# Loads of 48 rows for each head, gaps zeroed once, and another order of the work list

## The chip, the cores and the metric

The kernel runs on one core of a Trainium2 chip. Its engines work side by side, each through its own queue in order: TensorE (PE in the profile; its weight loads are PEld), VectorE (DVE), ScalarE (ACT), GpSimd (POOL) and SyncE (SP), which here issues most transfers. The metric is the device time of one execution in microseconds (us); the median of several runs counts.

## The reference

Two blocks follow each other. The first is a gated linear recurrence over 768 tokens, for 4 batches of 8 heads of 48 channels:

```python
f = 1.0 / (1.0 + np.exp(-f_logit))
for t in range(S):
    state = f[:, :, t, :, None] * state + np.einsum('bhd,bhe->bhde', k[:, :, t], v[:, :, t])
    y[:, :, t] = np.einsum('bhd,bhde->bhe', q[:, :, t], state)
```

The second takes y as x of shape (4, 768, 384), adds the real part of a Fourier transform over tokens and channels, and a two-layer perceptron on normalized rows:

```python
mixed = np.real(np.fft.fft(np.fft.fft(x, axis=1), axis=2))
u = x + mixed
un = (u - mean(u)) / np.sqrt(var(u) + 1e-06)      # over the channels
return u + np.maximum(un @ w_ch1, 0.0) @ w_ch2     # 384 -> 1536 -> 384
```

## The kernel before

Two heads of one batch make a unit u; there are 16 units, four to a batch. A unit's logits, keys and queries each lie in a buffer of 112 used partitions by 768 tokens (f32): 48 channels of head 0, a gap, and 48 channels of head 1 from partition 64. The buffers are four for logits (`g_t`), three for keys (`k_t`), four for queries (`q_t`), shared in turn by the units; some are parts of one tile called `wide`. Rows 48 to 63 belong to no head, but elementwise work and transposes run over all 112 rows, so something finite must lie there.

`attention` is a generator with 19 to 24 steps for a unit. For units 0 to 3: exponential of the logits on ScalarE (line 411); transposes on TensorE and logarithms on ScalarE (423, 425); running sums as a product with a triangle (433); the exponentials of the sums, g and W (439, 440), the decays te (458); query product (462) and key product (464) on VectorE; scores (472) and their masked copy (476); outputs within a block (631, 648, 652); state increments ds (673); the state scan stt on VectorE (681); its product with the queries (690); the way back to token rows (700 to 717), and the folding of tokens for the transform (739 to 767). Units 4 to 15 make the running sums with a scan on VectorE (449) instead. `keys_turned` (K, line 610) transposes the key products.

The weights arrive as 64-bit numbers in 24 blocks of 128 x 384 (128 x 768 words of four bytes). `fetch` (r, line 348) loads one into one of three buffers called `raw`; `weights` (C) makes single precision of it with one ScalarE, two VectorE and one GpSimd instruction (319, 321, 322, 323). `fnet` (F) is the transform of one batch, H the normalization and transposes, P the two layers of the perceptron: lines 927, 959, 968 and 982 are its products. V and c read weights a second time to look at their sizes, M judges whether the computation must be repeated in a safer form; for these inputs it is not.

The order of everything is written out by hand in `ORDER`, 970 words. Each word emits one step of one generator, or a load: `L1f` loads the logits of unit 1, `L4qv` queries and values of unit 4, a number n is the next step of unit n. As each engine runs its instructions in the order in which they were emitted, the list fixes every engine's queue, SP's included: a load that must wait for its buffer holds back all loads behind it.

How a load is made depends on the unit. For units 0 to 3, logits and queries come as 96 rows in one transfer (head 0, then head 1 from partition 48 on) and 16 more rows in a second one, which put the first 16 channels of head 1 on partitions 96 to 111; head 1 is thus turned by 16 rows, and the rows from 48 to 63 hold a copy. Keys of units 0 to 3 must be turned in the same way and take three transfers of 48, 32 and 16 rows. All loads of the units from 4 on are two transfers of 48 rows. VectorE zeroes rows 32 to 63 of the three key buffers ahead of the first load. The part of the file for the repeated computation (`few[0]` false) has loads of its own that stay.

Of the kernel before, what the change touches and what calls it, by code (L numbers as in the profile page):

```python
# [12 lines left out]
C = 128  # L13
# [11 lines left out]


ORDER = (
# [27 lines left out]
)  # L55


# [33 lines left out]
def kernel(  # L91
# [13 lines left out]
    nc = tc.nc  # L105
    B, HP, _, D, _, S = qkf.shape
# [8 lines left out]
    R = 64 + D  # L115
    ROWS = [slice(64 * r, 64 * r + D) for r in range(2)]
# [23 lines left out]
    few = [True]  # L140
# [7 lines left out]
    g_t = [fixed([128, S + 1], f"g{i}") for i in range(2)] + [wide_t[:, i * (S + 1):(i + 1) * (S + 1)] for i in range(2)]  # L148
    k_t = [fixed([128, S], f"k{i}") for i in range(2)] + [wide_t[:, 2 * S + 2:3 * S + 2]]
    q_t = [fixed([128, S], f"q{i}") for i in range(2)] + [wide_t[:, i * S + 2:(i + 1) * S + 2] for i in range(3, 5)]  # L150
# [72 lines left out]
    v_of, nulled = {}, []  # L223

    def load(u, *names):
# [3 lines left out]
        for name in names:  # L229
# [7 lines left out]
            rows = qkf.rearrange("b h r d i s -> (b h r d) i s")  # L237
            first = 2 * D * u
            if not nulled:
                nulled.extend(k_t)  # L240
                for a in k_t:
                    nc.vector.memset(a[32:64, :S], 0.0)
            if few[0] and (name == "k" or u >= HP):
                nc.sync.dma_start(out=t[:D, :S], in_=rows[first:first + D, i])
                first, turned = first + D, 16 if u < HP else 0
                nc.sync.dma_start(out=t[64:R - turned, :S], in_=rows[first + turned:first + D, i])
                if turned:
                    nc.sync.dma_start(out=t[R - turned:R, :S], in_=rows[first:first + turned, i])
                continue
            nc.sync.dma_start(out=t[:2 * D, :S], in_=rows[first:first + 2 * D, i])  # L250
            nc.sync.dma_start(out=t[2 * D:R, :S], in_=rows[first + D:first + 64, i])
# [968 lines left out]
```

## Time and profile before

| | us |
|---|---|
| median of 3 runs | 510.63 (510.14 to 513.66) |
| profiled execution | 512.57 |
| its span, first to last instruction | 510.8 |
| TensorE busy in the span | 485.5 |
| VectorE busy | 363.8 |
| ScalarE busy | 233.1 |
| GpSimd busy | 89.5 |
| mean granted TensorE clock | 0.993 |

The profiled execution's own time is 1.8 us above its span, and 1.94 us above the median of the runs. Busy times are sums over the whole span; engines overlap, and the share of an engine says nothing about one stage.

### The profile page before, as it was taken

Reading aid. Unit: us, or ns where it says so; the run is one execution under the profiler, and the core shown is the slowest. Engines: PE = TensorE matmul, PEld = TensorE weight load, DVE = VectorE, ACT = ScalarE, POOL = GpSimd, SP = SyncE. Lnnn points to the kernel's source line nnn. Section 1 sums busy time; section 2 is a strip of 40 time slices with the busy share of each in tenths; the row PEclk is TensorE's granted clock in tenths of the full one; section 3 lists DMA queues with packets and bytes.
Section 4 is the critical chain, followed back from the end, with each engine's and each line's share of the span. In section 5 each row is a group of like instructions: output and inputs, shape, how many; then the busy total and the mean of one; then the engine's idle time right before and its main releaser. Section 6 shows DMA issues by size and latency. Waiting matters only on the chain.

```text
span 510.8 us, 13829 instructions
## 1 busy us (share of the span) xinstructions
PE 485.5 (95%) x5806; PEld 450.2 (88%) x5806; DVE 363.8 (71%) x711; ACT 233.1 (46%) x552; POOL 89.5 (18%) x136
## 2 busy tenths in 40 slices
PE   4878889999999999999999999999999999999997
PEld 4766677886798999998998989999999999999997
DVE  2489988999959684585777886777486666558653
ACT  4688678866230541446463554452431413232130
POOL 2126632644222100000031000111000000010100
PEclk9799999999999999999999999999999999999999
DMA  8877946555201101113011112121200331134001
GB/s 225 236 210 192 248 144 206 170 174 155 83 1 47 38 3 37 43 54 103 30 48 37 49 43 59 58 57 41 98 1 15 110 124 63 62 138 143 31 3 38
DMA packets 20075, 46.20 MB, mean 90 GB/s; under 512 B 3489, under 2 KB 6242, under 8 KB 20002
## 3 DMA queue, kind: packets, MB, share of 16 engines
q1 hardware_dynamic: 18898, 41.66, 28.0%
q0 software_dynamic: 1104, 3.54, 1.9%
q8 instruction: 48, 0.79, 0.7%
q14 instruction: 25, 0.20, 0.1%
HBM read 40.47 MB, written 4.72 MB: 88 GB/s over the span
## 4 chain that ended last, share of the span: by engine, by line
PE 87%; DVE 4%; DMA 3%; ACT 2%; issue 2%; POOL 1%; SPq 0%; POOLq 0%; DVEq 0%; ACTq 0%
PE ub L927 26%; PE fx L982 17%; PE fz L982 12%; PE up L959 6%; PE y L631 3%; PE z L804 3%; PE po L968 3%; PE mix L824 2%; PE y L690 2%; PE ds L673 2%; PE sc L472 2%; PE pt L865 2%; DMA raw<-in_w_ch_dram 2%; PE yt L711 1%; PE run L433 1%
## 5 line engine op out<-in xcount | busy, mean ns | idle before, releaser
L936 DVE TENSOR_TENSOR h<-h,ub 128x512 f32<-128x512 f32 x90 | 61.0, 686 | 32.4 <-PE ub L927 24.7
L934 ACT ACTIVATE h<-ub 128x512 f32<-128x512 f32 x60 | 35.6, 593 | 51.9 <-PE ub L927 50.6
L772 POOL DMA_INDIRECT out_dram<-x,place x16 | 21.3, 1332 | 179.8 <-DVE x L1040 124.3
L927 PE MATMUL ub<-wide,w 128*128 128x128 f32 x400 | 49.8, 276 | 1.7 <-DVE wide L899 1.7
L927 PEld LDWEIGHTS ub<-wide,w 128*128 128x128 f32 x400 | 47.3, 192 | 2.4 <-DVE wide L899 1.6
L939 ACT ACTIVATE h<-h 128x512 f32<-128x512 f32 x50 | 31.1, 632 | 35.2 <-DVE h L936 35.2
L982 PE MATMUL fx<-block,h 128*128 128x192 f32 x264 | 46.7, 327 | 0.0
L982 PE MATMUL fx<-w,h 128*128 128x192 f32 x264 | 45.6, 328 | 0.0
L982 PEld LDWEIGHTS fx<-block,h 128*128 128x128 f32 x264 | 43.4, 190 | 0.2
L982 PEld LDWEIGHTS fx<-w,h 128*128 128x128 f32 x264 | 42.6, 190 | 0.2
L927 PE MATMUL ub<-unT,w 128*128 128x128 f32 x320 | 41.0, 275 | 0.0
L927 PEld LDWEIGHTS ub<-unT,w 128*128 128x128 f32 x320 | 38.4, 192 | 0.0
L323 POOL TENSOR_TENSOR w<-w,raw 128x384 uint32<-128x384 uint32 x24 | 27.7, 1161 | 56.7 <-ACT raw L319 18.7
L959 PE MATMUL up<-unT,w 128*128 128x256 f32 x144 | 33.2, 384 | 0.1
L927 PE MATMUL ub<-wide 128*128 128x128 f32 x240 | 31.9, 276 | 0.9 <-DVE wide L899 0.9
L927 PE MATMUL ub<-unT,wide 128*128 128x128 f32 x240 | 32.2, 277 | 0.0
L866 ACT COPY unT<-pt 128x384 f32<-128x384 f32 x24 | 11.4, 476 | 42.2 <-PE pt L865 42.0
L959 PEld LDWEIGHTS up<-unT,w 128*128 128x128 f32 x144 | 26.7, 190 | 4.3 <-DVE x L887 0.4
L927 PEld LDWEIGHTS ub<-wide 128*128 128x128 f32 x240 | 29.4, 192 | 1.2 <-PE ub L927 1.1
L927 PEld LDWEIGHTS ub<-unT,wide 128*128 128x128 f32 x240 | 29.2, 192 | 0.4
L982 PE MATMUL fz<-block,h 128*128 128x192 f32 x132 | 23.5, 328 | 0.0
L476 DVE COPY_PREDICATED at<-causal,sc 128x768 f32<-128x768 uint32 x16 | 16.6, 1040 | 9.3 <-PE sc L472 8.0
(216 smaller groups left out, 1011.4 us busy)
## 6 DMA issues: line engine op xcount, KB each, us to landing
raw<-in_w_ch_dram SPq DMA_DIRECT2D x24, 384.0 KB, 5.1
v<-in_v_dram SPq DMA_DIRECT2D x16, 288.0 KB, 3.8
k<-in_w_ch_dram SPq DMA_DIRECT2D x12, 384.0 KB, 3.6
g<-in_w_ch_dram SPq DMA_DIRECT2D x12, 384.0 KB, 4.1
k<-in_qkf_dram SPq DMA_DIRECT2D x25, 144.0 KB, 3.4
g<-in_qkf_dram SPq DMA_DIRECT2D x20, 144.0 KB, 4.6
q<-in_qkf_dram SPq DMA_DIRECT2D x20, 144.0 KB
wide<-in_qkf_dram SPq DMA_DIRECT2D x11, 144.0 KB, 4.3
```

The costliest lines, as they stand in the source:

```text
L323: nc.gpsimd.tensor_tensor(bits, bits, lo, ALU.add)
L476: nc.vector.copy_predicated(AT, causal[:, :64].bitcast(U32).unsqueeze(1).unsqueeze(1).to_broadcast([128, 2, NCH, 64]), own[:, :, :NCH * 64 ...
L631: nc.tensor.matmul(y[FILL[g], c // 3, c % 3 * C + t.start:c % 3 * C + t.stop], lhsT=vals[rows, o:o + (64 if g == 0 else D)], rhs=weights, ...
L772: nc.gpsimd.indirect_dma_start(out=out.rearrange("b s d -> (b s) d"), out_offset=bass.IndirectOffsetOnAxis(ap=place[:, b, i:i + 1], axis=0 ...
L804: nc.tensor.matmul(z[:, cols], lhsT=src[:, j, lo:hi], rhs=tab[:, t, T % 2, cols], start=(i == 0), stop=(i == len(parts) - 1), skip_group_c ...
L927: nc.tensor.matmul(chains[chain][:, m * 128:(m + 1) * 128], lhsT=block(w)[:, m * 128:(m + 1) * 128], rhs=tokens(a), start=(new and m == 0) ...
L934: nc.scalar.activation(out, got, kind, scale=1.0 if how == "=+" else -1.0)
L936: nc.vector.tensor_tensor(out, out, got, ALU.add if how == "+" else ALU.subtract)
L939: nc.scalar.activation(out, out, AF.Relu)
L959: nc.tensor.matmul(pp[:, :256], lhsT=w1[:, kt, m * 128:(m + 1) * 128], rhs=unT[:, kt], start=(kt == 0), stop=(kt == 2))
L968: nc.tensor.matmul(po[:, :DM], lhsT=h[:, m, t], rhs=w2[:, m], start=(m == 0), stop=(m == NF - 1))
L982: nc.tensor.matmul(out, lhsT=h[:, m], rhs=blocks[i][:, m], start=(start and m == 0), stop=(m == H - 1), skip_group_check=True)
```

## The change

All loads of units (in the normal computation) become two transfers of 48 rows, one for each head, on partitions 0 to 47 and 64 to 111. Head 1 is no longer turned. Rows 32 to 63 of all eleven buffers are zeroed by VectorE, in an order of their own, ahead of the first load.

```diff
             if not nulled:
-                nulled.extend(k_t)
-                for a in k_t:
+                nulled.extend((g_t[0], g_t[1], q_t[0], g_t[2], k_t[1], k_t[0], q_t[1], g_t[3], q_t[2], k_t[2], q_t[3]))
+                for a in nulled:
                     nc.vector.memset(a[32:64, :S], 0.0)
-            if few[0] and (name == "k" or u >= HP):
-                nc.sync.dma_start(out=t[:D, :S], in_=rows[first:first + D, i])
-                first, turned = first + D, 16 if u < HP else 0
-                nc.sync.dma_start(out=t[64:R - turned, :S], in_=rows[first + turned:first + D, i])
-                if turned:
-                    nc.sync.dma_start(out=t[R - turned:R, :S], in_=rows[first:first + turned, i])
+            if few[0]:
+                for r in range(2):
+                    nc.sync.dma_start(out=t[ROWS[r], :S], in_=rows[first + r * D:first + (r + 1) * D, i])
                 continue
```

The list `ORDER` holds the same 970 words, each as often as before, in another sequence throughout. Its beginning, which the prediction speaks of:

```diff
-    "I L1f L0f i L0v E 1 0 0 1 0 0 L0k r C 0 1 1 0 L0q 0 0 1 L2f 2 L1q 0 Z 0 K0 0 0 r 2 2 r 1 L1k 1 L3fk "
-    "L2q 0 0 2 1 0 0 1 3 1 L2k C C 2 L1v 0 3 3 K1 L4fk 0 1 0 2 L3q 3 1 1 1 2 2 4 1 0 1 3 3 3 L3v 1 2 3 2 "
+    "E r i L1f L0f 0 r 1 r L2f 0 1 0 I L0q 2 0 0 1 L0v Z 2 C 0 L0k 0 1 1 L1v L1q 0 L3fk 1 L1k 0 0 K0 C "
+    "L2q C 0 3 2 2 1 0 1 r L2k L3q L4fk 0 2 0 0 K1 3 3 0 1 2 2 3 1 0 1 C 1 3 1 1 2 2 4 1 1 2 3 3 0 1 4 3 "
```

I sets constants on GpSimd, E the triangle, i loads the 128 x 128 identity, Z zeroes the score buffers. In the old list the first P0 is word 220, behind ten C and 146 steps of units; in the new one it is word 214, behind nine C and 144 steps.

## Rows read from the trace of the kernel before

**Rows 1.** The page: busy time of each engine, and the chain by engine.
```profile
PE 485.5 (95%) x5806; PEld 450.2 (88%) x5806; DVE 363.8 (71%) x711; ACT 233.1 (46%) x552; POOL 89.5 (18%) x136
...
PE 87%; DVE 4%; DMA 3%; ACT 2%; issue 2%; POOL 1%; SPq 0%; POOLq 0%; DVEq 0%; ACTq 0%
```
**Rows 2.** Busy time by stretch: start, end, length, engines, clock, transfer share, GB/s.
```profile
0.00:7.18 7.18, 0.00 (x0) 0.00 (x0) 2.09 (x3) 3.15 (x5) 2.96 (x21) 1.00 0.70 193
7.18:28.00 20.82, 18.84 (x297) 16.67 (x297) 7.51 (x10) 14.06 (x32) 3.29 (x12) 0.84 0.92 243
28.00:57.00 29.00, 23.36 (x777) 20.18 (x777) 27.60 (x43) 22.84 (x56) 16.16 (x27) 1.00 0.74 205
57.00:85.00 28.00, 23.57 (x473) 18.97 (x473) 24.70 (x47) 21.38 (x62) 9.88 (x10) 1.00 0.66 187
85.00:507.30 422.30, 419.74 (x4260) 394.37 (x4260) 301.54 (x610) 171.63 (x402) 57.22 (x66) 1.00 0.22 67
507.30:511.00 3.70, 0.03 (x1) 0.00 (x0) 0.36 (x1) 0.00 (x0) 0.00 (x0) 1.00 0.29 86
```
**Rows 3.** The same view in stretches of 2 us around the slow clock.
```profile
14.00:16.00 2.00, 1.43 (x52) 1.26 (x52) 0.97 (x2) 1.61 (x4) 1.22 (x10) 1.00 1.05 323
16.00:18.00 2.00, 1.29 (x20) 0.90 (x9) 1.68 (x2) 1.67 (x4) 0.00 (x0) 0.70 1.03 243
18.00:20.00 2.00, 2.00 (x52) 1.86 (x52) 1.15 (x2) 0.94 (x2) 0.00 (x0) 0.50 1.03 233
20.00:22.00 2.00, 2.00 (x49) 1.72 (x51) 0.00 (x0) 1.62 (x5) 0.00 (x0) 0.50 0.75 194
22.00:24.00 2.00, 2.00 (x39) 1.66 (x32) 0.22 (x1) 1.60 (x4) 0.00 (x0) 0.59 0.84 233
```
**Rows 4.** TensorE's largest wait (28 to 90 us), and P0's first products in the timeline.
```profile
PE y L690 <- DVE stt L681: 4.7, 6, 1.3
...
84.97 1.56 PE L959 MATMUL up<-unT,w 128*128 128x256 f32 x6
```
**Rows 5.** Timeline of VectorE: start, length, line, operation, idle before and releaser.
```profile
1.03 1.50 DVE L242 MEMSET k<- 32x768 f32 x2 [1.03 <-PEq L1206]
...
10.83 0.36 DVE L321 TENSOR_SCALAR w<-raw 128x384 uint32<-128x384 uint32 x1 [7.49 <-DMA raw<-in_w_ch_dram]
...
14.20 0.96 DVE L464 TENSOR_TENSOR g<-W,k 112x768 f32<-112x768 f32 x1 [0.19 <-DVE q L462]
...
23.78 0.76 DVE L681 TENSOR_TENSOR_SCAN stt<-ds,te 112x288 f32<-112x288 f32 x1 [4.18 <-PE ds L673]
26.91 1.04 DVE L476 COPY_PREDICATED at<-causal,sc 128x768 f32<-128x768 uint32 x1 [2.37 <-PE sc L472]
27.84 0.35 DVE L321 TENSOR_SCALAR w<-raw 128x384 uint32<-128x384 uint32 x1
...
30.38 0.95 DVE L462 TENSOR_TENSOR wide<-wide 112x768 f32<-112x768 f32 x1
```
**Rows 6.** Timeline of the first 13 us: SP, ScalarE and TensorE.
```profile
1.26 0.42 SPq L251 DMA_DIRECT2D g<-in_qkf_dram  x1
...
4.25 0.84 ACT L411 ACTIVATE g<-g 112x768 f32<-112x768 f32 x1 [2.15 <-DMA g<-in_qkf_dram]
...
6.20 0.84 ACT L411 ACTIVATE g<-g 112x768 f32<-112x768 f32 x1 [1.01 <-DMA g<-in_qkf_dram]
...
7.18 2.28 PE L423 MATMUL pg<-ident,g 112*128 112x112 f32 x10 [7.18 <-ACT g L411]
...
12.12 0.90 ACT L439 ACTIVATE g<-run,rise 112x768 f32<-112x768 f32 x1 [0.57 <-PE run L433]
```
**Rows 7.** Transfer queues over the whole span: transfers, MB, share.
```profile
q1 hardware_dynamic: 18898, 41.66, 28.0%
```
**Rows 8.** Busy time by stretch while loads of 48 + 48 rows land.
```profile
121.00:122.00 1.00, 1.00 (x20) 0.88 (x16) 1.00 (x3) 0.00 (x0) 0.57 (x1) 1.00 1.03 271
122.00:123.00 1.00, 1.00 (x4) 0.60 (x4) 0.96 (x2) 0.48 (x1) 0.54 (x1) 1.00 1.01 264
```

50 rows, old and new, of the table ORDER are left out of this document.

## The prediction

> **What bounds the kernel now.** I read the page's busy times and its chain first [rows 1]. TensorE is busy 485.5 us of a span of 510.8 us, and 87% of the chain that ended last lies on it. So the time is TensorE's work plus its idle time, and the diff leaves the count and shapes of its matmuls alone: only the 25.3 us of idle time, and the clock at which the work runs, can move. The busy times by stretch [rows 2] say where the 25.3 us lie: 7.18 us before its first instruction; 20.82 - 18.84 = 1.98 us up to 28 us; 29.00 - 23.36 = 5.64 us from 28 to 57 us; 28.00 - 23.57 = 4.43 us from 57 to 85 us; 422.30 - 419.74 = 2.56 us from 85 us to the last product; and some 3.5 us of stores behind it. Nearly all that can be won or lost lies ahead of 85 us, where the first projection (P0) begins, at 84.97 us [rows 4].
>
> Within that, from 28 to 57 us VectorE is busy 27.60 of 29.00 us, and TensorE's largest wait is for VectorE's state scan (stt, line 681), 4.7 us in six places from 28 to 90 us [rows 4]. Between 10 and 28 us VectorE is anything but full (7.51 of 20.82 us): it sits 4.18 us before its first state scan and 2.37 us before the copy at 26.91 us, then runs the vector halves of the second and third weight conversion (C) from 27.84 to 30.38 us, already in its full stretch [rows 5]. The very start waits for loads: ScalarE's first exponential begins at 4.25 us, the second at 6.20 us, and TensorE behind it at 7.18 us [rows 6]. The transfers are nearly saturated there (share 0.92 at 243 GB/s, [rows 2]).
>
> **The change, part by part.** *Bytes and transfers.* Eight loads (logits and queries of the first four units) were 96 + 16 rows and become 48 + 48. Each row is 768 x 4 = 3072 bytes, so 8 x 16 rows = 393 KB go. Four key loads go from three transfers to two at equal bytes. At 243 GB/s the bytes are 1.6 us of a stream that after 28 us no waiting TensorE instruction names; I count them only at the start (below) and otherwise at 0, with -1.6 as the other end. The four transfers saved are four issues of about 0.42 us on SP [rows 6]; nobody was seen waiting for SP's issue itself, so 0.
>
> *Zeroing.* Three fills of 32 x 768 become eleven. Two took 1.50 us [rows 5], so eight more are 6.0 us, from 1.03 us to about 9.3 us. VectorE's next work was at 10.83 us, when a weight block landed, so the cover is idle time and the cost 0; without that cover it would be up to 6 us. The new wait is SP's: a load must wait for its buffer's fill. The first load (logits of unit 1, second in the list of fills) may be issued at 1.03 + 1.50 = 2.53 us instead of 0.81 us, and all that SP holds is queued behind it. But a weight block (128 x 768 words, 393 KB) and the identity (128 x 128 words, 66 KB) are now queued ahead of it, and 459 KB keep the transfer engines past 2.53 us, so this costs nothing on top of the next item (bare, it would be +1.7 us).
>
> *The first loads behind a weight block.* Before, the second logits load (344 KB) landed about 1.95 us after the first (ScalarE starts at 4.25 and 6.20 us, [rows 6]), that is 176 KB per us. 459 KB ahead, less 2 x 49 KB no longer loaded, is 361 KB, or 2.0 us at that rate and 1.5 us at 243. Unit 0's exponential comes first in the new list, but its logits are the second to land, so TensorE starts at about 7.18 + 2.0 = 9.2 us, and the exponentials of the running sums, at 12.12 us before [rows 6], come at about 14. I take **+2.0** (ends +1.5 and +2.5; the nearest row is that of the same two loads).
>
> *Two more blocks before the third logits.* Two further weight blocks are now fetched before unit 2's logits, whose exponential stands ahead of unit 0's second set on ScalarE. By that point 2.13 MB are asked for; at 243 GB/s from about 2.2 us they are there at 11.0 us, while unit 0's logarithms end near 12. Cost 0; the other end is +1.
>
> *Keys of unit 1.* They are now queued on SP behind keys of unit 3, which wait until VectorE has used unit 0's keys (its product, 14.20 us before, ends near 17.2). Two loads of 295 KB then take 2.4 us plus about 2 us to land, so they are there at 21.8 us. In the new list VectorE first does the copy of unit 0, two weight conversions and unit 1's query product, and gets there at about 22. Cost 0, the other end +1.
>
> *What fills VectorE's gap.* In the new list the second and third conversion stand before unit 1's products, that is, in the idle stretch up to 27 us, where 4.18 + 2.37 = 6.55 us were idle. They need only blocks that were fetched at the very start. They took 30.38 - 27.84 = 2.54 us of the full stretch, which then begins earlier: **-2.5** (bounds 0, if the lag eats the gap, and -2.5). Unit 2's query product, 0.95 us at 30.38 us, also moves ahead of unit 1's copy, into the wait for the scores: **-0.95** (bounds 0 and -0.95). What is late next is the state scan of unit 0, whose product on TensorE carries the lag of 2.0 us.
>
> *The rest of the list.* P0 first stands at word 214 instead of 220 of 970, with nine conversions before it instead of ten and 144 attention steps instead of 146. So the stage that keeps TensorE full starts with slightly less done; the work is only deferred. After 85 us the idle time before the tail is 2.56 us [rows 2]; another sequence may lose it or double it: 0, with ends -2.6 and +2.6.
>
> *Sum.* +2.0 - 2.5 - 0.95 = -1.45 us. The profiled execution was 512.57 us with a span of 510.8, so 1.8 us lie around the span: 509.35 of span, 511.1 profiled. The median of the runs shown, 510.63, is 1.94 us below the profiled one, which gives **509.2 us**.
>
> *A rule that speaks against the loads.* In rows, the 96 + 16 loads ran at 243 and 233 GB/s between 16 and 20 us with the transfer engines full [rows 3]. From 121 to 123 us, when 48 + 48 loads of units 8 to 11 are what is left in flight, the rate is 271 and 264 GB/s at full share [rows 8]. So 48-row pieces are not slower. The Trainium skill, page SBUF — State Buffer, section "Door 1: The DMA port swizzle", says that a transfer reaching only partitions 0 to 63 (or only 64 to 127) reaches half of the 16 ports and so half the bandwidth; by it each new piece would go at half rate where a 96-row piece spanned both halves. The trace does not bear that out at these rates.
>
> **The rivals.** *The clock (slower).* The granted clock was 0.70, 0.50, 0.50 and 0.59 in the four stretches from 16 to 24 us: the lower of the two levels, 1.2 GHz, after TensorE had been busy only 1.43 and 1.29 of 2 us; it rose again after it had been busy throughout from 18 us [rows 3]. That is 8 x (1 - 0.57) = 3.4 us of work lost. If the later and sparser start (waits for logits, for the third exponential) gives a second such stretch, or one twice as long, and the lag is not repaid, the time is 510.6 + 2.0 + 3.4 = 516.0. It decides if TensorE is not continuously busy by about 24 us. Against it: the three units in flight then give it as much work as before.
>
> *The lag stays.* Scores, sums and scans of unit 0 all come 2 us later and VectorE's gap only moves: 510.6 + 2.0 = 512.6, up to 514.6 if the keys of unit 1 and the third logits cost 1 us each. For it: VectorE has a single order, and what stands before a late scan cannot pass it.
>
> *The lead grows (faster).* VectorE's full stretch sets TensorE's 5.64 + 4.43 = 10.07 us of idle time from 28 to 85 us. If the new order halves it, on top of the sum's -1.45, the time is 510.6 - 1.45 - 5.0 = 504.2. For it: the largest wait there is for VectorE's scan. Against it: VectorE's work ahead of P0 stays the same but for a conversion, and 27.60 of 29.00 us leave it little to compress.
>
> *Half-rate pieces.* If the 48-row pieces ran at half of 243 GB/s, eight loads of 295 KB would take 19.4 us instead of 8 x 344 KB in 11.3 us: +8 us, in a stretch whose transfers are saturated, so about 518.7 at worst. This is the page's rule put as a mechanism of this kernel; rows 8 speak against it.
>
> *The loads change nothing.* If the old filler rows cost nothing and the zeros hide fully, only the list remains, and that is inside the forecast.
>
> **How the numbers follow.** Forecast (lag repaid, 506 to 512): 0.48. Lag stays (512 to 515): 0.17. Clock: 0.13. Half-rate pieces: 0.02. Lead grows: 0.20. The predicted time is that of the first, 509.2 us. The range leaves out about a tenth on either side, half of the clock case with the half-rate case and half of the faster case: 504.2 to 515.5. A measurement of this kernel tells about 1% (505.5 to 515.7) from no change. Faster by more than that: 0.20, all from the growing lead. Slower: 0.15, the clock and the half-rate pieces. Same: 0.65.
>
> **What would show it.** In the changed profile: eleven fills on VectorE to about 9 us; the first logits exponential near 8 us and TensorE's first instruction near 9.2 us; two conversions on VectorE before its first state scan; VectorE's sum from 28 to 57 us still above 27 us; P0's first matmul (line 959) within 2 us of 84.97 us [rows 4]; queue 1 moving 41.66 - 0.39 = 41.27 MB [rows 7]; 1.2 GHz for no more than about 8 us. The prediction is wrong if P0 begins more than 4 us away from there, or if TensorE's idle time after 85 us moves by more than 3 us: then the sequence, which I could only bound, outweighs the start that I worked out.

## The result, and the profile after

| | before | after |
|---|---|---|
| median, us | 510.87 (508.96 to 515.67, 22 runs) | 513.72 (511.12 to 518.17, 22 runs) |
| ratio, after to before | | 1.005 [1.0028, 1.0072] |
| profiled execution, us | 512.57 | 513.28 |
| its span, us | 510.8 | 511.6 |
| its mean granted clock | 0.993 | 0.989 |

The changed kernel is slower by 0.5%, some 2.6 us (1.4 to 3.7 by the interval). The forecast was 509.2 us, 0.3% faster. The time lies in the range that was given, and within the 1% that was called "same", but on the other side of no change than the sum of -1.45 us. Ratios and means of runs here and below leave out every run more than 1.5% above the fastest of its kernel, among them three that stand far off, at 630.31 us (conversions_back), 712.81 us (before_held) and 2777.74 us (before).

The two profiled executions show only 0.7 of these 2.6 us, since that of before was 1.7 us above its median and that of after 0.4 below. So the traces show what happened in each stretch, and the repeated runs what it cost. Line numbers after are three lower than before (L439 is now L436, L690 is L687, L959 is L956).

The page after, as in [rows 1] and [rows 7]: busy times, the granted clock in 40 slices of 12.8 us, queue 1, and the chain by engine.

```profile
PE 486.4 (95%) x5806; PEld 449.9 (88%) x5806; DVE 366.0 (72%) x719; ACT 233.3 (46%) x552; POOL 87.5 (17%) x136
...
PEclk9799899999999999999999999999999999999999
...
q1 hardware_dynamic: 18706, 41.27, 28.4%
...
PE 84%; ACT 4%; DMA 4%; DVE 4%; issue 2%; SPq 2%; POOL 0%; ACTq 0%; DVEq 0%; POOLq 0%
```

The clock is below full in the second slice and again in the fifth, from 51 to 64 us. Queue 1 moves the 41.27 MB that were forecast; the bytes that went bought nothing that can be seen. The busy times by stretch, in the stretches of [rows 2]:

```profile
7.18:28.00 20.82, 16.04 (x228) 14.12 (x229) 10.69 (x16) 14.62 (x30) 4.06 (x3) 0.84 0.90 233
28.00:57.00 29.00, 25.13 (x830) 21.48 (x829) 25.00 (x41) 23.33 (x60) 13.86 (x17) 1.00 0.74 197
57.00:85.00 28.00, 24.94 (x490) 19.62 (x485) 24.38 (x46) 22.76 (x62) 12.50 (x18) 0.94 0.63 178
85.00:507.30 422.30, 419.50 (x4267) 394.19 (x4266) 300.16 (x613) 171.35 (x402) 51.78 (x67) 1.00 0.23 68
507.30:512.00 4.70, 0.76 (x5) 0.46 (x3) 0.36 (x1) 0.00 (x0) 0.00 (x0) 0.89 0.23 68
```

Read them against [rows 2]. Up to 28 us TensorE does 16.04 us instead of 18.84. From 28 to 57 us VectorE falls from 27.60 to 25.00 us of 29.00, where above 27 was forecast: it is no longer full, it waits. From 57 to 85 us the clock is 0.94, where it was 1.00. TensorE's idle time up to 507.3 us is 7.18 + 4.78 + 3.87 + 3.06 + 2.80 = 21.7 us against 21.8 before, so in this pair idle time was only moved, and the difference is 0.84 us more of busy time, with a mean clock of 0.989 against 0.993. Idle time after 85 us moved by 0.24 us.

The start after, ScalarE's and TensorE's timeline, against [rows 6]: first logits, first transposes, logits of unit 2, exponential of unit 0's sums.

```profile
7.56 0.84 ACT L408 ACTIVATE g<-g 112x768 f32<-112x768 f32 x1 [5.47 <-DMA g<-in_qkf_dram]
...
8.55 2.28 PE L420 MATMUL pg<-ident,g 112*128 112x112 f32 x10 [8.55 <-ACT g L408]
...
13.74 0.84 ACT L408 ACTIVATE wide<-wide 112x768 f32<-112x768 f32 x1 [2.51 <-DMA wide<-in_qkf_dram]
14.58 0.88 ACT L436 ACTIVATE g<-run,rise 112x768 f32<-112x768 f32 x1
```

The exponential of unit 0's sums starts at 14.58 us, 2.46 us later than at 12.12. ScalarE stood 2.51 us for the logits of unit 2, which land at about 13.7 us and not at 11.0. Up to there the transfers ran at 248 GB/s at a share of 0.92, as fast as before (0.92 and 243 GB/s in [rows 2]):

```profile
2.20:13.70 11.50, 4.73 (x24) 4.20 (x24) 7.54 (x12) 3.12 (x7) 3.73 (x22) 1.00 0.92 248
```

VectorE's timeline, against [rows 5]:

```profile
6.68 3.12 DVE L242 MEMSET wide<- 32x768 f32 x4
9.84 0.36 DVE L318 TENSOR_SCALAR w<-raw 128x384 uint32<-128x384 uint32 x1
...
17.35 0.96 DVE L461 TENSOR_TENSOR g<-W,k 112x768 f32<-112x768 f32 x1 [0.90 <-DMA k<-in_qkf_dram]
...
20.40 0.35 DVE L318 TENSOR_SCALAR w<-raw 128x384 uint32<-128x384 uint32 x1
...
21.65 0.56 DVE L319 SCALAR_TENSOR_TENSOR w<-raw,w 128x384 uint32<-128x384 uint32 x1
22.12 0.95 DVE L459 TENSOR_TENSOR q<-q,g 112x768 f32<-112x768 f32 x1
24.10 1.63 DVE L461 TENSOR_TENSOR g<-W,k 112x768 f32<-112x768 f32 x1 [1.03 <-DMA k<-in_qkf_dram]
27.60 0.76 DVE L678 TENSOR_TENSOR_SCAN stt<-ds,te 112x288 f32<-112x288 f32 x1 [1.88 <-PE ds L670]
28.28 0.93 DVE L459 TENSOR_TENSOR wide<-wide 112x768 f32<-112x768 f32 x1
30.50 1.05 DVE L473 COPY_PREDICATED at<-causal,sc 128x768 f32<-128x768 uint32 x1 [1.29 <-PE sc L469]
...
35.20 0.76 DVE L678 TENSOR_TENSOR_SCAN stt<-ds,te 112x288 f32<-112x288 f32 x1 [1.95 <-PE ds L670]
```

The fills end at 9.8 us. The second and third conversion run from 20.40 to 22.2 us, ahead of the first state scan, as forecast. But the first scan comes at 27.60 us instead of 23.78, and with the copy that ends at 30.50 + 1.05 = 31.55 us VectorE has done the same work that it had done at 30.38 + 0.95 = 31.33 us before. What was moved forward has just paid for the lag. Then it stands 1.95 us for unit 1's scan, at 35.20 us: the conversions that filled this place before are used up. The same scan in the kernel before came 1.88 us earlier and hardly waited:

```profile
33.32 0.76 DVE L681 TENSOR_TENSOR_SCAN stt<-ds,te 112x288 f32<-112x288 f32 x1 [0.30 <-PE ds L673]
```

The lag also grows on its way: 1.37 us at the first transposes, 2.46 us at the exponential of the sums, 3.15 us at unit 0's key product (17.35 against 14.20 us) and 3.82 us at the first scan. At the key product VectorE waits 0.90 us for unit 0's keys themselves, for which SP issues the load at 10.49 us, where it was issued at 4.20 us before. In every profile TensorE's first scores start 0.10 us behind this product.

The clock, in stretches of 2 us (columns as in [rows 3]):

```profile
16.00:18.00 2.00, 0.90 (x6) 0.49 (x5) 1.10 (x2) 2.00 (x7) 0.24 (x1) 1.00 0.97 253
18.00:20.00 2.00, 1.14 (x49) 1.03 (x50) 0.84 (x2) 1.91 (x4) 1.18 (x1) 0.87 0.57 161
20.00:22.00 2.00, 2.00 (x45) 1.72 (x48) 1.93 (x5) 1.31 (x3) 0.00 (x0) 0.50 0.98 239
22.00:24.00 2.00, 2.00 (x27) 1.88 (x21) 1.07 (x2) 2.00 (x6) 1.72 (x2) 0.50 0.74 152
24.00:26.00 2.00, 2.00 (x26) 1.75 (x28) 1.63 (x1) 0.55 (x2) 0.91 (x1) 0.50 0.89 300
...
58.00:60.00 2.00, 0.24 (x8) 0.24 (x12) 1.97 (x4) 1.46 (x3) 1.99 (x7) 1.00 0.99 227
60.00:62.00 2.00, 2.00 (x22) 1.12 (x19) 2.00 (x2) 1.05 (x5) 1.77 (x4) 0.61 1.03 235
```

TensorE, busy 0.90 and 1.14 of 2 us, falls to the lower level (1.2 GHz) at about 19.5 us and stays there until about 26.3 us. A second such stretch, new against before, follows a pause at 58 to 60 us, in which it works 0.24 us and waits 1.92 us for a state scan:

```profile
59.76 1.01 PE L687 MATMUL y<-q,stt 48*48 48x128 f32 x20 [1.92 <-DVE stt L678]
```

### The profile page after: what moved, and what is told of

It reads as the page before. It is cut to its first block, busy times and chain, and to the rows that moved or that the text cites. A ratio compares the mean times of both kernels' runs of the same rounds, so it can differ in the third digit from the quotient of the medians.

```text
span 511.6 us, 13832 instructions
## 1 busy us (share of the span) xinstructions
PE 486.4 (95%) x5806; PEld 449.9 (88%) x5806; DVE 366.0 (72%) x719; ACT 233.3 (46%) x552; POOL 87.5 (17%) x136
## 3 DMA queue, kind: packets, MB, share of 16 engines
q1 hardware_dynamic: 18706, 41.27, 28.4%
## 4 chain that ended last, share of the span: by engine, by line
PE 84%; ACT 4%; DMA 4%; DVE 4%; issue 2%; SPq 2%; POOL 0%; ACTq 0%; DVEq 0%; POOLq 0%
PE ub L924 27%; PE fx L979 17%; PE fz L979 12%; PE z L801 4%; PE up L956 4%; PE po L965 3%; PE y L628 3%; PE mix L821 3%; PE y L687 2%; DMA wide<-in_qkf_dram 2%; PE ds L670 2%; PE yt L708 1%; PE sc L469 1%; PE pt L862 1%; PE st L607 1%
## 5 line engine op out<-in xcount | busy, mean ns | idle before, releaser
L769 POOL DMA_INDIRECT out_dram<-x,place x16 | 16.5, 1029 | 210.5 <-DVE x L1037 88.4
L956 PE MATMUL up<-unT,w 128*128 128x256 f32 x144 | 32.7, 383 | 0.6 <-DVE x L884 0.6
L956 PEld LDWEIGHTS up<-unT,w 128*128 128x128 f32 x144 | 26.9, 190 | 4.9 <-PE yt L708 0.8
L863 ACT COPY unT<-pt 128x384 f32<-128x384 f32 x24 | 11.5, 478 | 42.9 <-PE pt L862 42.9
L979 PE MATMUL fz<-w,s 128*128 128x192 f32 x132 | 23.4, 327 | 0.0
```

Source lines behind the costliest of these rows:

```text
L769: nc.gpsimd.indirect_dma_start(out=out.rearrange("b s d -> (b s) d"), out_offset=bass.IndirectOffsetOnAxis(ap=place[:, b, i:i + 1], axis=0 ...
L956: nc.tensor.matmul(pp[:, :256], lhsT=w1[:, kt, m * 128:(m + 1) * 128], rhs=unT[:, kt], start=(kt == 0), stop=(kt == 2))
L979: nc.tensor.matmul(out, lhsT=h[:, m], rhs=blocks[i][:, m], start=(start and m == 0), stop=(m == H - 1), skip_group_check=True)
```

## The experiments

Each ratio is to runs of the kernel before on the same chip, where its medians were 510.39 to 511.13 us in the groups of runs below; the ratio on record isn't the quotient of the medians, and the two differ by up to 0.4%. The theories under test: **A**, the start, the weight blocks ahead of the first and third logits and the lag behind them; **E**, VectorE's gap only moved, so that the moved conversions are worth nothing; **F**, the clock, 1.2 GHz more often because TensorE works more sparsely; **H**, the wait of the first loads for the fills; **I**, the loss lies in the first part of the new list. Where an expectation uses other letters, they stand for rivals that it describes itself.

**The two halves of the change.** loads_alone has the loads and fills of after with the list of before, list_alone the reverse.

```diff
 # loads_alone: lines 237 to 247 of after, ORDER of before
 # list_alone: ORDER of after, load() of before
```

> The new loads and the eleven fills under the old list. Theory A (the cost comes from the new list: two weight blocks ahead of unit 2's logits, and TensorE's pause at 58 us): the loads cost only what the first fill holds back, 1.7 us less 98 KB saved, about +1 us at the start, most of it taken up later: 510.5 to 512 us, ratio below 1.003. Theory B (the loads themselves cost, by a lower rate of 48-row pieces or by the fills): 512.5 us or more, ratio 1.004 or more, with loads of one unit seen to take longer than 344 KB did before.

> The new list with the old loads (96 + 16 rows, three fills). Theory A: slower than before by 2 to 4 us, ratio 1.004 to 1.008, as 393 KB more are moved under the same order; ScalarE waits for unit 2's logits 2.5 us or more at about 11 us. Theory B: no different from before, ratio 0.998 to 1.002.

Measured: 512.78 us, 1.0056 [1.0031, 1.0081], and 515.27 us, 1.0089 [1.0057, 1.0121]. Each half costs, and they don't add up: under the new list, the new loads go with a lower time, 513.7 against 515.27 us. In loads_alone A, by which the loads cost next to nothing, was to give a ratio below 1.003, and failed. Without a weight block ahead of it, the first load's wait for the fills lies open; ScalarE of loads_alone, as in [rows 6]:

```profile
5.95 0.84 ACT L408 ACTIVATE g<-g 112x768 f32<-112x768 f32 x1 [3.85 <-DMA g<-in_qkf_dram]
```

5.95 against 4.25 us is the 1.7 us that the prediction gave as the bare cost of the fills. In list_alone the first exponential starts at 7.50 us, as late as after, so the late start as such belongs to the list. But the logits of unit 2 start ScalarE at 12.43 us after a wait of 1.26 us, where 2.5 us or more were expected, and the exponential of unit 0's sums comes at 13.27 us, later by 1.15 us and not by 2.46.

**Single places of the new list.** logits_first asks for unit 2's logits ahead of the two weight blocks. state_first moves unit 4's steps ahead of unit 3's before word S, so that the scan that TensorE waited for at 59.76 us comes earlier. conversions_back returns the second and third conversion behind unit 1's masked copy.

```diff
 logits_first
-E r i L1f L0f 0 r 1 r L2f 0 1 0 I
+E r i L1f L0f L2f 0 r 1 r 0 1 0 I
 state_first
-K4 7 5 3 3 S 4 4 4 4 6 5 4 F0
+K4 7 4 4 5 4 3 3 S 4 6 5 4 F0
 conversions_back
-K0 C L2q C 0 3 2 2 ... 3 3 0 1 2 2 3 1 0 1 C
+K0 L2q 0 3 2 2 ... 3 3 0 1 2 2 3 1 C C 0 1 C
```

> The changed kernel with unit 2's logits asked for ahead of the two further weight blocks, all else as it is. Theory A: ScalarE's third exponential no longer waits until 13.74 us but starts near 11, unit 0's exponentials of the sums come 1.5 to 2.5 us earlier (14.58 us in the changed kernel), and the time falls by 1 to 2 us, to a ratio of 1.001 to 1.003. Rival C (what is lost at the start is taken up by 57 us anyway, since VectorE then sets the pace): the wait goes and the time stays at 1.005.

> The changed kernel with unit 4's state scan moved ahead of unit 3's folding on VectorE (and its state increments ahead of unit 5's scores on TensorE). Theory A: TensorE's pause from 57.8 to 59.8 us goes or shrinks below 0.5 us, the clock of 0.61 and 0.54 from 60 to 64 us with it, and the time falls by 1 to 2 us, to a ratio of 1.001 to 1.003. Rival D (the pause only moves: what the folding delays is late instead): the time stays at 1.005 and the slow clock turns up elsewhere ahead of 85 us.

> The changed kernel with the second and third weight conversion moved from VectorE's first gap to behind unit 1's masked copy, near where the old list has them. The forecast's step (they cost nothing in the first gap and 2.5 us later): 2 to 2.5 us slower than the changed kernel, ratio 1.009 to 1.010. Theory E (the gap only moved: VectorE idles from 33.2 to 35.2 us in the changed kernel because the work that used to fill it is gone): no slower, ratio 1.003 to 1.007, and VectorE's idle time from 28 to 57 us falls by 1.5 us or more.

Measured: 1.0056 [1.0029, 1.0082], 1.0074 [1.0049, 1.01] and 1.0037 [1.0006, 1.0068]. None is told apart from the changed kernel's 1.005. In logits_first ScalarE did not wait for unit 2's logits (first row), but the exponential of unit 0's sums came at 13.87 us, only 0.71 us earlier where 1.5 to 2.5 were expected. The first scan came at 25.04 us without idle time, 2.6 us earlier; this lead isn't the logits' alone, as the granted clock of this profile is 1.00 up to 28 us, against 0.84 in the profile after. The second scan came where it was, after 4.20 us of idle time:

```profile
11.48 0.84 ACT L408 ACTIVATE wide<-wide 112x768 f32<-112x768 f32 x1
...
25.04 0.76 DVE L678 TENSOR_TENSOR_SCAN stt<-ds,te 112x288 f32<-112x288 f32 x1
...
35.20 0.76 DVE L678 TENSOR_TENSOR_SCAN stt<-ds,te 112x288 f32<-112x288 f32 x1 [4.20 <-PE ds L670]
```

What is won at the first scan is stood off at the next. The trace shows on what: ahead of the second scan TensorE stops for 1.88 us inside a group of scores, and no engine and no transfer of data is named as what released it.

```profile
29.90 0.32 PE L645 MATMUL sc<-q,g 48*64 48x64 f32 x7
32.10 0.47 PE L645 MATMUL sc<-q,g 48*64 48x64 f32 x17 [1.88 <-issue]
```

Such pauses inside a group stand ahead of 60 us in 12 of the 16 profiles, 22 in all, of 0.17 to 2.94 us. In TensorE's stream, products and weight loads counted together, they lie at six positions, 450, 705, 961, 1217, 1473 and 2241 (or the one behind), which are 256 or a multiple of it apart, give or take one. Each ends 1.27 to 1.63 us after a packet of the instruction queue has landed (q8 on the page: 48 packets, 0.79 MB, so 16 KB each). So TensorE most likely stands here for its own program code; that is read from the traces, and no run tests it. The pause above is at position 705. Its packet lands at 30.67 us here and at 31.00 us after, where TensorE gets to that place at 32.36 us and no pause shows. As long as this packet comes when it does, an earlier first scan can't bring the second one much forward. Without dummy products the pauses add up to 0.7 us in the mean over five profiles with the old beginning of the list and to 1.2 us over seven with the new one; single profiles reach from 0 to 2.94 and from 0 to 2.35, so the two aren't told apart.

In state_first the expected wait shrank from 1.92 to 0.34 us, and the clock was 1.00 from 56 to 66 us; but the stretch at 1.2 GHz turned up from about 43 to 47 us instead, behind such a pause of 1.52 us, and the time was no lower. Its rival D came true:

```profile
42.88 0.33 PE L628 MATMUL y<-at,v 64*64 64x64 f32 x5 [1.52 <-issue]
...
61.29 0.91 PE L687 MATMUL y<-q,stt 48*48 48x128 f32 x20 [0.34 <-DVE stt L678]
```

```profile
44.00:46.00 2.00, 2.00 (x61) 1.78 (x61) 0.83 (x2) 0.98 (x2) 0.50 (x1) 0.50 0.99 229
```

In conversions_back VectorE's timeline shows the idle time back ahead of unit 1's keys, and the second scan 2.1 us later still, at no cost in time:

```profile
25.92 0.96 DVE L461 TENSOR_TENSOR g<-W,k 112x768 f32<-112x768 f32 x1 [2.81 <-DMA k<-in_qkf_dram]
28.28 0.76 DVE L678 TENSOR_TENSOR_SCAN stt<-ds,te 112x288 f32<-112x288 f32 x1 [1.40 <-PE ds L670]
...
37.33 0.74 DVE L678 TENSOR_TENSOR_SCAN stt<-ds,te 112x288 f32<-112x288 f32 x1
```

So E holds in the time: by the two intervals (1.0037 [1.0006, 1.0068] against 1.005 [1.0028, 1.0072]) the two conversions aren't worth the 2.5 us that the prediction booked, though a gain of some 1 us isn't excluded. E's other sign, 1.5 us less idle time of VectorE from 28 to 57 us, was narrowly missed: 4.00 us became 2.67. A isn't borne out as a cause in a single place: its waits are real, but in each of these runs taking one away moved the wait, not the end.

**The clock held by dummy products.** A word D emits eight products of 128 x 128 bf16 into an unused part of a bank (line 219), used by no later step.

```diff
 clock_held (after)
-E r i L1f L0f 0 r 1 r L2f 0 1 0 I L0q 2 0 0 1 L0v Z 2 C 0 L0k 0 1 1 L1v L1q 0 L3fk 1 L1k 0 0
+E I D D D D D D r i L1f L0f 0 r 1 r L2f 0 1 0 L0q 2 0 0 1 D D L0v Z 2 C 0 L0k 0 1 D D 1 L1v L1q 0 L3fk 1 L1k 0 D 0
 ... and D D D behind unit 4's twelfth step
 before_held (before)
-I L1f L0f i L0v E 1 0 0 1 0 0 L0k r C 0 1 1 0 L0q 0 0 1 L2f 2 L1q 0 Z
+I L1f L0f i L0v E D D D D D D 1 0 0 1 0 0 L0k r C 0 1 1 D 0 L0q 0 0 1 L2f 2 L1q 0 D Z
```

> The changed kernel with 14 groups of eight dummy products on TensorE where it idles (six ahead of the first logits, the rest near 13, 17, 19 and 58 us), and the constants one place earlier; the output stays the same. Theory F (a part of the loss is the clock: TensorE's idle stretches at 12 to 20 and 58 to 60 us bring the 1.2 GHz stretches behind them): mean granted clock 0.997 or more where the changed kernel had 0.992 on average, and the time falls by about 1.5 us, to a ratio of 1.002 to 1.003. Rival G (the clock is a by-product; TensorE waits for VectorE there anyway): clock up and time the same, 1.005.

> The kernel before with eight such groups (six ahead of the first logits, one at 15 us, one at 16 us). Theory F: its clock, 0.997 on average in the last runs, has little to give: 0 to 1 us faster, ratio 0.998 to 1.000, and the runs below 0.995 go. Rival G: the same within 0.2%, or slower by what the groups delay, 0.5 us.

Measured: clock_held 511.80 us, 1.0024 [1.0, 1.0048]; before_held 515.98 us, 1.0099 [1.0064, 1.0133]. The stretches of clock_held:

```profile
7.18:28.00 20.82, 15.30 (x300) 13.37 (x300) 12.70 (x17) 15.61 (x33) 4.88 (x3) 1.00 0.94 235
28.00:57.00 29.00, 24.38 (x817) 20.49 (x813) 24.09 (x39) 22.67 (x58) 13.18 (x16) 1.00 0.71 188
57.00:85.00 28.00, 25.20 (x509) 20.11 (x505) 24.58 (x45) 22.63 (x62) 12.08 (x18) 1.00 0.63 186
```

The clock is 1.00 in all three in this profile, and the ratio is half of the changed kernel's loss, although the dummies themselves are TensorE work (busy time up to 489.3 us). That is in line with F for the changed kernel, as a part; it isn't shown by the time, as the intervals 1.0024 [1.0, 1.0048] and 1.005 [1.0028, 1.0072] overlap, and the mean clock over the runs rose from 0.993 to 0.996, short of the 0.997 expected. In the kernel before the same means made things worse, with a mean clock over its runs of 0.991 against 0.996 without them. That was not expected, and stays open.

**The start, and the order of the halves.** upper_first is loads_alone with the transfer to partitions 64 to 111 issued first (the fills touch only rows 32 to 63, so it waits for none) and unit 1's logits buffer filled first. start_mended does the same in the changed kernel, and asks for all three logits ahead of the weight blocks and the identity but the first block. before_again and after_again are the two kernels unchanged.

```diff
 upper_first, start_mended
-nulled.extend((g_t[0], g_t[1], q_t[0], ...
+nulled.extend((g_t[1], g_t[0], q_t[0], ...
-    for r in range(2):
+    for r in (1, 0):
 start_mended
-E r i L1f L0f 0 r 1 r L2f 0 1 0
+E L1f L0f i L2f 0 r 1 r r 0 1 0
```

> The old list with the new loads, head 1's half ahead of head 0's in each load and unit 1's logits buffer zeroed first, so that SP's first transfer need not wait for a fill. Theory H (the loads alone cost 2 us because the first fill holds SP back by 1.7 us and the whole start follows): the first exponential comes near 4.5 us instead of 5.95, TensorE starts near 7.3 instead of 8.2 us, ratio 0.999 to 1.002. Rival (the fills or the 48-row transfers cost elsewhere): the start is earlier and the ratio stays near 1.005.

> The kernel before unchanged, for a second profile of it and as a control: ratio 1.000 within 0.3%. Theory F (the clock differs between executions, and a slow stretch costs about 0.6 us per us of clock lost): at a mean clock of 1.000 in its records it takes 509.5 us, at 0.993 about 511.6.

> The changed kernel unchanged, for a second profile and a tighter ratio: 1.003 to 1.007. Theory F: its mean clock is again near 0.992 against 0.997 of the kernel before, which is about half of the difference; at the same clock it is about 2 us slower than before.

> The changed kernel with the first three logits loads ahead of all weight blocks, head 1's half ahead of head 0's and unit 1's logits buffer zeroed first. Theory H (the late start is the cause in the changed kernel too): first exponential near 4.5 us instead of 7.56, TensorE from about 7 us, unit 0's exponentials of the sums near 11.5 instead of 14.58, ratio 0.999 to 1.002. Rival I (the order of the units' steps behind the start is the cause, the start only a part): the start moves by 2 to 3 us and the ratio stays at 1.003 or more.

Measured: upper_first 1.0022 [0.9994, 1.0051], before_again 0.9997 [0.9962, 1.0033], after_again 1.0057 [1.0034, 1.0081], start_mended 514.06 us, 1.0083 [1.0056, 1.011]. For the loads alone H is borne out in the trace: with the wait for the fills hidden, ScalarE starts at 4.53 us again. The loss is no longer told from zero, but nor is it told from that of loads_alone, [1.0031, 1.0081]. In the changed kernel the same start, with the logits first, brought the first exponential to 5.98 us (4.5 was expected), the first transposes from 8.55 to 6.97 us, and the exponential of unit 0's sums to 11.84 us, earlier than in the kernel before; and the time did not fall:

```profile
6.97 2.28 PE L420 MATMUL pg<-ident,g 112*128 112x112 f32 x10 [6.97 <-ACT g L408]
...
26.06 0.76 DVE L678 TENSOR_TENSOR_SCAN stt<-ds,te 112x288 f32<-112x288 f32 x1 [1.68 <-PE ds L670]
```

2.74 us won at the exponential are 1.5 us at the first scan and 0.5 us at the second, which comes at 34.66 us. Two losses on the way show in the trace: VectorE's first key product waits 1.96 us for unit 0's keys, which are still asked for at 8.19 us (4.20 before), and TensorE makes its pause at position 705, here of 0.98 us:

```profile
15.69 1.16 DVE L461 TENSOR_TENSOR g<-W,k 112x768 f32<-112x768 f32 x1 [1.96 <-DMA k<-in_qkf_dram]
...
31.85 0.47 PE L645 MATMUL sc<-q,g 48*64 48x64 f32 x17 [0.98 <-issue]
```

What the other runs lost behind these places can't be read from this trace: its execution took 511.69 us, 2.4 us less than the median. The mean clock over its runs is 0.989, the lowest of all kernels. In its profile the stretches up to 28 us and from 57 to 85 us have the same clock as in the changed kernel, 0.84 and 0.94.

**The list, cut in two.** old_start has the loads of before and its list up to word W, the 346th, and what is left in the order of the new list.

```diff
 old_start
-... L11qv P0 P0 P0 P0 W 6 P0 4 4 P0 P0 ...
+... L11qv P0 P0 P0 P0 W 8 4 6 4 7 7 P0 P0 P0 B B ...
```

> The old loads, the old list up to the word W (346 words, to about 110 us) and the new list's order for all words left. Theory I (the new list loses in its first part alone and is as good or better behind it): 0.998 to 1.001. Rival J (the new list's loss lies behind W): 1.004 or more.

Measured: 510.67 us, 0.9973 [0.9935, 1.0011]. I holds: none of the list's loss is seen behind W, so it lies in about the first fifth of the time. The order behind W is as good as the old one within the noise; that it is better is not shown.

**What eats the mended start.** mended_held is start_mended with dummy products in the sparse places alone, held_58 the changed kernel with three D behind unit 4's twelfth step alone. There the first dummy opens a bank in which outputs within a block are being summed, so part of these sums is changed in held_58; the amount of work isn't.

```diff
 mended_held
-E L1f L0f i L2f 0 r 1 r r 0 1 0 I L0q 2 0 0 1 L0v
+E I L1f L0f i L2f 0 r 1 r r 0 1 0 L0q 2 0 0 1 D D L0v
 ... and D as in clock_held behind it; held_58: D D D behind unit 4's twelfth step
```

> The mended start with eight dummy products of TensorE in the sparse places (two after unit 1's third step, two after its fourth, one after unit 0's ninth, three after unit 4's twelfth), none ahead of the first logits. If the slow clock ate what the mended start brings (clock theory): the mean granted clock rises from 0.9886 to 0.995 or more and the ratio to the kernel before falls from 1.0083 to 1.003 or below (1.002 at equal clock). If the new list gives the lead back in VectorE's order behind the start (schedule theory): the ratio stays at 1.006 to 1.010, whatever the clock.

> The changed kernel with three dummy products alone, after unit 4's twelfth step, where TensorE pauses at 58 to 60 us and then ran at 1.2 GHz. If that pause carries the clock's part: the stretch from 57 to 85 us shows a granted clock of 1.00 and the ratio falls from 1.005 to about 1.003. If the sparse start from 12 to 20 us carries it: the ratio stays at 1.005, and the stretch of 1.2 GHz before 28 us is still there.

Measured: mended_held 513.51 us, 1.0061 [1.0025, 1.0097], mean clock 0.993; held_58 514.43 us, 1.0059 [1.003, 1.0087], mean clock 0.994. In mended_held the clock rose from 0.989 three quarters of the way to the 0.995 that was asked for, and the ratio from 1.0083 only to 1.0061, where the clock theory had 1.003: this lies in the range of the other theory, but the intervals overlap, so neither is shown. In held_58 no gain is seen, and its profile meets neither expectation, as the clock in it is 1.00 up to 28 us and below 1.00 behind 57. The stretch of 57 to 85 us in held_58, with TensorE busier than in any other kernel, and its clock lower:

```profile
57.00:85.00 28.00, 26.91 (x561) 22.50 (x562) 24.14 (x47) 22.48 (x60) 11.73 (x18) 0.89 0.58 171
...
58.00:60.00 2.00, 2.00 (x52) 1.72 (x55) 1.91 (x6) 1.69 (x3) 1.58 (x2) 0.50 0.78 230
```

The slow stretch came here before the dummies, which start at 62.8 us: where it falls differs between executions. So held_58 doesn't test whether a clock held from 58 us on would help.

**All runs together.** The runs of the two kernels in all groups, by the mean granted clock of the run: mean time in us, with the number of runs.

| clock of the run | before | after |
|---|---|---|
| 0.999 and above | 509.3 (53) | 512.4 (3) |
| 0.995 to 0.998 | 511.1 (26) | 512.7 (10) |
| 0.991 to 0.994 | 512.1 (27) | 514.1 (9) |
| 0.990 and below | 514.6 (8) | 514.6 (12) |

46% of the runs of before have full clock, and 9% of those of after; the means are 0.9964 and 0.9927. A straight line through these runs of all kernels (one constant for each kernel) gives 0.66 us of time for each us of clock lost. By it, (0.9964 - 0.9927) x 512 x 0.66, or some 1.2 us of the 3.0 us between the two means of the times are clock, and some 1.7 us remain at equal clock. The lines of the table differ by 3.1, 1.6, 2.0 and 0 us, so one slope fits them badly and the split is rough.

## Why the prediction went as it did

**The bound** was read rightly: TensorE's work is as before, idle time after 85 us moved by 0.24 us, and what was lost was lost ahead of 85 us. P0's first product came at 82.6 us instead of 84.97, 2.4 us early and so outside the 2 us that were given; its last, at 149.7 us, came 2.5 us late against 147.2. The start of a stage that is fed piece by piece was a poor mark; its end was the better one. Three other signs came out: the fills ended at 9.8 us (9 was said), the first exponential started at 7.56 us (8), TensorE at 8.55 us (9.2). Two failed: VectorE's busy time from 28 to 57 us, and 1.2 GHz for about 8 us at most, as the two slow stretches lose 3.3 and 1.7 us, so last some 10.

**Bytes, transfers** at 0: right. For the half-rate pieces see [rows 3]: the stream that holds them ran at 253 GB/s at a share of 0.97 from 16 to 18 us, against 243 GB/s in those 2 us before. The trace after disagrees again with the Trainium skill, page SBUF — State Buffer, section "Door 1: The DMA port swizzle", by which each piece on one side of partition 64 would have half the bandwidth.

**Zeroing** at 0, with +1.7 us if bare: right in both. In the new list a weight block covers it; in loads_alone it lies bare and the first exponential is 1.70 us late, which upper_first takes away.

**First loads behind a block**, +2.0 (1.5 to 2.5): the mechanism was right. The lag was 1.37 us at the first transposes and 2.46 us at the exponentials of the sums.

**Third logits** at 0, end +1: undersized. They landed at 13.7 us and not at 11.0, and 2.51 us of ScalarE's time went into the wait. The estimate took 243 GB/s from 2.2 us on, and the rate was right: the transfers ran at 248 GB/s from 2.2 to 13.7 us. What was short are the bytes. At this rate 2.85 MB moved in these 11.5 us, where the estimate had 2.13 MB; it left out the loads of unit 0 that SP issues from 6.2 us on and that share the transfer engines. **Keys of unit 1** at 0, end +1: the end came, 1.03 us of wait. But logits_first shows that taking away the third logits' wait alone did not lower the time. **Keys of unit 0** have no term at all: they were put at the lag of 2 us, without a look at where the new list asks for them. Asked for at 10.49 us, they hold VectorE 0.90 us, and the key product is 3.15 us late. No run tests what this is worth.

**What fills VectorE's gap**, -2.5 and -0.95: this is the step that failed. The order came out as forecast, but the saving counted only if the next scan was ready earlier, and it was ready later. The prediction's own rival said it: "VectorE's gap only moves". By 31.5 us both kernels have done the same VectorE work; then the new one stands where the old one had conversions left to do, and VectorE's busy time from 28 to 57 us fell to 25.00 us. conversions_back takes the conversions out of the gap and is no slower. So the sum is left with its +2.0 us, which is near the 2.6 us measured, and 513.7 us lies in the 512 to 515 that the prediction gave to its rival of the lag. That is in part luck: some 1.2 of the 2.6 us go with the clock, and the two kernels that took away a part of the early lag or all of it, logits_first and start_mended, were no faster.

**The clock**, a rival with 0.13, was priced as +3.4 us on top of the whole lag, and seems to have come in part: a second slow stretch at 60 us, in the profiles of after, after_again, conversions_back and start_mended alike (0.94 from 57 to 85 us). All the clock that the changed kernel has less is some 1.2 us in the mean. The prediction let the clock be all or nothing, and took the one stretch of 1.2 GHz in its profile for a property of the kernel before; 46% of that kernel's runs have a mean clock of 0.999 or more, so hardly any of it.

**The rest of the list** at 0: right behind W, within the noise (old_start).

What stays open: which words ahead of W cost the 1.7 us at equal clock (taking back one place alone, as in logits_first, state_first and conversions_back, did not give them back), where start_mended's median loses what its earlier start won, and why dummy products hurt the kernel before (before_held's profile shows 2.65 us of pauses inside groups). The late keys of unit 0 and the pauses of TensorE inside its groups are rivals that the traces show and no run tests.

## What to carry to other kernels

Work moved into an engine's idle gap pays only if what ends the gap comes no later; if the same edit delays that, the gap reopens where the moved work had been, so ask what fills the old place. When a load is asked for later, look at every product that uses it, and not only at those that waited before. Before a stretch at the lower clock goes into a sum, see in how many of the kernel's runs it occurs. When many buffers are zeroed ahead of their first loads, zero first the buffer that is loaded first, and issue first the piece that touches no zeroed row.

## What the runs showed of the hardware

The granted clock is no property of a kernel: over 114 runs of before the mean of a run was 0.983 to 1.000, and runs at 0.990 and below took 514.6 us against 509.3 at full clock, 1.0% more. The Trainium skill, page TensorE: Matmul & The Clock Gate, section "Part 1: The HAM clock gate", says that the slow part at the start varies between runs of the same kernel; these runs agree, and show one behind a pause as late as 58 us.

The clock column does not tell the speed of TensorE's first products. Ten first transposes took 2.28 us in the kernel before [rows 6], and in before_held, behind 48 dummy products, eight took 0.98 us (122 ns each against 228), while the column reads 1.00 in both:

```profile
1.92 5.30 PE L219 MATMUL y<-bound 128*128 128x128 bf16 x48 [1.92 <-POOL bound L188]
7.20 0.98 PE L423 MATMUL pg<-ident,g 112*128 112x112 f32 x8
```

The last store's time varies: from its issue to the end of the span 3.0 us in the profile of before (507.81 to 510.8) and 5.1 us in that of mended_held, whose last store was issued at 505.91 us and whose span is 511.0. In 11 of the 16 profiles it is 3.0 to 3.1 us, in the others 3.5 to 5.1. So some 2 us between two executions can come from there alone.
